# One kernel, two orders: engines that issue in the order of the text, and a triangular solve that moves to GpSimd while VectorE rounds the weights

## The chip, the core and the metric

The kernel runs on one core of a Trainium2 chip. That core has five engines that work side by side and meet at semaphores: TensorE (PE; its weight loads are shown as PEld), VectorE (DVE), ScalarE (ACT), GpSimd (POOL) and SyncE (SP), which here only issues DMA transfers. ACT issues some too. The metric is the device time of one execution in microseconds (us), as the median of several runs. Lower is better.

## What is computed

The first part is a recurrence over time, for 4 batches and 8 heads with 768 steps and 40 channels, that keeps a 40 x 40 state per batch and head. The second part is a feed-forward layer (FFN) over the 3072 tokens that come out of it, 320 to 2048 to 320 channels, with a squared ReLU.

```python
for t in range(S):                                    # B=4, H=8, S=768, D=40
    y[:, :, t] = einsum('bhd,bhde->bhe', rt, state)
    Sa = einsum('bhde,bhe->bhd', state, at)
    state_decay = state * wt[:, :, None, :] - einsum('bhd,bhe->bhde', Sa, bt)
    state = state_decay + einsum('bhd,bhe->bhde', vt, kt)
x = y.transpose(0, 2, 1, 3).reshape(B * S, H * D)     # 3072 x 320
h = maximum(x @ w_in, 0.0)                            # w_in 320 x 2048
out = (h * h @ w_out).astype(float32)                 # w_out 2048 x 320
```

The two weights arrive in 64 bits and are rounded to 32 bits in the kernel, with integer operations on VectorE.

## The kernel before

**Chunks and rounds.** Time is cut into chunks of 128 steps, so that a batch has 6 chunks and all batches 24. The kernel goes through them with the chunk number outside and the batch inside: chunks 0 to 3 are the first chunk of each of the four batches and are called round 0 here, chunks 4 to 7 are round 1, and so on to round 5. Within a chunk, the recurrence becomes matrix products and the inverse of a triangular matrix per head; between chunks of one batch only the state is carried.

**Four kinds of work.** `early(i)` (L224 to L246) prepares a chunk: transposes of w, b and a on PE (`turn`, L202), running products of the decays on VectorE (L229, L230) with their reciprocals (L232, L233), the decayed b and a (L238, L239), and a product `N` of the two (L77) that ACT copies (L244). Everything it makes is written to DRAM, by DMAs of SP (`kept_up`, `kept_down`, `kept_a`, `kept_n`). `solve(c)` (L250 to L275) makes the triangular inverses of a whole round at once. It loads the two 64 x 64 diagonal blocks of N of every head into `half_n`, with one DMA for 8 heads (16 DMAs in all, L262), so that each of 128 partitions holds half a problem. Then come 63 steps of two element-wise operations (a product L268 and a subtraction L270), each step needing the one before, and two DMAs write the result to `kept_t` (L274). `rest(i)` (L278 to L316) prepares what a chunk needs just ahead of its turn: it reads the kept decays and `a` back (L283 to L288), transposes k, r and v, makes the masked products A and RV (L218), and loads the inverse `T` (two DMAs, L314) and a block of `N` (L315). `chain(i)` (L322 to L399) is the serial part: it scales the state by four small VectorE operations (L329 to L332), transposes it on PE (L336), and goes through some seven matmul groups with ACT copies between them, then updates the state (L376) and writes the output `tokens` (L395). Four small DMAs (L398) bring the last heads' channels together. Before that, `load(i)` has SP fetch k, r, v and b (L113).

**The FFN.** `ffn()` takes the tokens of two chunks at once (a group), 12 groups in all. A group has 16 steps of three matmuls 128x256 (`ps_f<-tokens,w_in`), each followed by a ReLU on ACT (L415) and a product on VectorE (L416, `hid`), and 8 steps of four matmuls 128x320 (`ps_f<-w_out,hid`). A group's steps fill the time of PE between the links of the chain of the next two chunks.

**Rounding the weights.** `rounded` (L153 to L172) fetches a piece of 64-bit weights through ACT's DMA queue (L158) into one of two buffers, after POOL has cleared it where the piece doesn't fill it (L156), and turns it into 32 bits with 9 VectorE operations (L163 to L172). There are 24 pieces of 128x256 for `w_in` and 16 of 128x320 for `w_out`.

**Order.** The text makes four early chunks, then solve(0) on VectorE woven with the early work of chunks 4 to 7, then solve(1) on POOL, and then the loop over chunks. In a loop turn, the steps of chain(i), rest(i+1), early(i+8) and the FFN are emitted in turns by `weave`. After the last chunk of round c comes solve(c+2) on POOL. The order of the text is not the order of issue: each engine's instructions are sorted by a scheduler before the program is built. A DMA that SP issues waits at its place in SP's order for its data and its buffer, and what stands behind it waits too.

Of the kernel before, what the change touches and what calls it, by code (L numbers as in the profile page):

```python
# [17 lines left out]
def kernel(  # L18
# [22 lines left out]
    nc = tc.nc  # L41
    B, H, S, D = r.shape
# [96 lines left out]
    middle = lambda t_: t_[:, :, MID:MID + 1]  # L139
    ups = Ring("up", 1, [128, NP, C + 2], 1.0, middle)  # L140
    downs = Ring("down", 1, [128, NP, C + 2], 1.0, middle)
    minus_x = Ring("minus_x", 2, [128, H, DP], 0.0, pads)
    states = Ring("state", B, [128, NP, 2, DP], 0.0, lambda t_: t_)

    w_in = single("w_in", [128, NT, DFF])
    w_out = single("w_out", [128, NF, DM])

# [4 lines left out]
    def rounded(dst, srcs):  # L152
        raw = work.tile([128, WP, 2], I32, tag="raw", name="raw")[:, :dst.shape[-1]]  # L153
        n = 128
        if sum(m_ for _, m_, _ in srcs) < n:
            nc.gpsimd.memset(raw, 0)  # L156
        for row, m_, src in srcs:
            nc.scalar.dma_start(out=raw[row:row + m_].rearrange("p f e -> p (f e)"), in_=src.bitcast(I32))  # L158
        lo, hi = raw[:, :, 0].bitcast(U32), raw[:, :, 1]
        power = work.tile([128, WP], I32, tag="power", name="power", bufs=1)[:n, :dst.shape[-1]]  # L160
        p_ = work.tile([128, WP], I32, tag="signed", name="signed", bufs=1)[:n, :dst.shape[-1]]
        bits = dst.bitcast(I32)
        nc.vector.tensor_scalar(power, hi, 20, 0x7FF, Alu.logical_shift_right, Alu.bitwise_and)  # L163
# [4 lines left out]
        nc.vector.tensor_scalar(bits, hi, 0xFFFFF, 3, Alu.bitwise_and, Alu.logical_shift_left)  # L168
# [5 lines left out]
    WP = 320  # L174
    WI = 256
# [350 lines left out]
```

## Time and profile before

| What | Value |
|---|---|
| Three runs | 1544.03, 1536.1 and 1532.33 us, median 1536.1 |
| The profiled execution: its own time | 1534.04 us |
| The profiled execution: its span in the trace | 1532.3 us |
| Mean granted PE clock | 0.786 of full speed |
| DMA traffic | 123.01 MB, mean 80 GB/s |
| Solves on POOL | 315 products and 315 subtractions (5 solves of 63 steps) |

The span is the time from the first to the last instruction of the profiled execution; its own time is 1.7 us longer. In the profile, "busy" is the time in which an engine has an instruction in work. A line with 40 digits shows the busy share of an engine in 40 slices of the span, 38.3 us each, in tenths. A row of the timeline gives the start, the duration, the engine, the line of the code, the operation, its output and inputs, and, in brackets, the idle time of the engine just before it and what ended it. "SPq" is the time in which SP issues a DMA. The table of windows gives the busy time of each engine in a stretch, with the number of its instructions, then the granted PE clock, the busy share of the DMA engines and their GB/s.

### The profile page before, as it was taken

How to read it: one execution, taken by the hardware profiler on the slowest of the kernel's cores; microseconds unless marked ns; L12 is line 12 of the kernel's file. 1: busy time of each engine (PE TensorE's matmuls, PEld its weight loads, DVE VectorE, ACT ScalarE, POOL GpSimd, SP SyncE). 2: the span in 40 equal slices, each digit the busy share in tenths (PEclk: the TensorE clock that was granted, in tenths of full speed). 3: DMA queues.
4: the chain of work that ended last, by engine and by line, in shares of the span. 5: the costliest groups of instructions: out<-in, count | busy, mean ns of one | idle time of the engine just before them, and what ended most of it. 6: DMA issues, size and time to landing. Idle time of an engine off the chain costs nothing.

```text
span 1532.3 us, 18790 instructions
## 1 busy us (share of the span) xinstructions
PE 1062.4 (69%) x7248; PEld 884.2 (58%) x7248; DVE 598.7 (39%) x1330; ACT 202.1 (13%) x453; POOL 566.7 (37%) x702
## 2 busy tenths in 40 slices
PE   3300025009975989649989769899399994499999
PEld 2200014008854878537878658788278784388877
DVE  5887699604623243212135321346031342022311
ACT  0000001001210211101202101112012111021211
POOL 2110000009990079920199700499500899100000
PEclk9555555556897996859967878959799887699999
DMA  9634694374606677063846185654447640422100
GB/s 172 153 69 88 100 163 89 62 58 88 111 1 125 64 133 130 0 114 64 90 85 116 25 135 61 79 112 77 84 81 61 102 77 2 79 63 50 29 11 9
DMA packets 389881, 123.01 MB, mean 80 GB/s; under 512 B 318752, under 2 KB 372896, under 8 KB 389792
## 3 DMA queue, kind: packets, MB, share of 16 engines
q1 hardware_dynamic: 384000, 111.32, 45.6%
q10 hardware_dynamic: 5792, 10.49, 3.1%
q8 instruction: 57, 0.93, 0.3%
q14 instruction: 32, 0.26, 0.1%
HBM read 79.00 MB, written 41.78 MB: 79 GB/s over the span
## 4 chain that ended last, share of the span: by engine, by line
POOL 36%; PE 32%; DMA 11%; DVE 10%; SPq 7%; issue 4%; ACTq 0%; ACT 0%; DVEq 0%; POOLq 0%
PE ps_f L77 19%; POOL half_t L270 19%; POOL half_p L268 17%; PE ps_c L77 8%; PE ps_w L77 2%; DMA raw<-in_moe_w_in_dram 2%; SPq L262 2%; DMA in_k<-in_k_dram 2%; DMA raw<-in_moe_w_out_dram 2%; DVE half_t L270 2%; DVE half_p L268 2%; PE ps_w L202 2%; SPq L274 1%; SPq L398 1%; DMA kept_down<-down 1%
## 5 line engine op out<-in xcount | busy, mean ns | idle before, releaser
L268 POOL TENSOR_TENSOR half_p<-half_n,half_t 128x462 f32<-128x462 f32 (+46 forms) x315 | 255.6, 811 | 397.3 <-DMA in_k<-in_k_dram 176.1
L270 POOL TENSOR_TENSOR half_t<-half_t,half_p 128x462 f32<-128x462 f32 (+46 forms) x315 | 281.7, 894 | 24.7
L77 PE MATMUL ps_f<-tokens,w_in 128*128 128x256 f32 x1152 | 288.3, 399 | 0.5 <-DVE hid L416 0.5
L77 PEld LDWEIGHTS ps_f<-tokens,w_in 128*128 128x128 f32 x1152 | 217.7, 197 | 34.0 <-issue 1.5
L77 PE MATMUL ps_f<-w_out,hid 128*128 128x320 f32 x768 | 220.7, 441 | 0.0
L416 DVE TENSOR_TENSOR hid<-ps_f,hid 128x256 f32<-128x256 f32 x192 | 81.2, 423 | 319.2 <-ACT hid L415 319.0
L77 PEld LDWEIGHTS ps_f<-w_out,hid 128*128 128x128 f32 x768 | 144.4, 192 | 57.4 <-issue 3.0
L202 PE MATMUL ps_w<-ident,in_k 128*128 128x128 f32 x96 | 20.1, 342 | 151.0 <-DMA in_k<-in_k_dram 150.9
L77 PE MATMUL ps_c<-xr,T 64*64 64x40 f32 x768 | 65.8, 249 | 81.4 <-DMA T<-kept_t 74.5
L415 ACT ACTIVATE hid<-ps_f 128x256 f32<-128x256 f32 x192 | 73.6, 383 | 346.5 <-PE ps_f L77 346.5
L77 PEld LDWEIGHTS ps_c<-xr,T 64*64 64x64 f32 x768 | 59.1, 159 | 96.4 <-DMA T<-kept_t 75.0
L202 PEld LDWEIGHTS ps_w<-ident,in_k 128*128 128x128 f32 x96 | 14.2, 178 | 155.0 <-DMA in_k<-in_k_dram 117.7
L202 PE MATMUL ps_w<-ident,in_w 128*128 128x128 f32 x96 | 22.2, 376 | 113.9 <-DMA in_w<-in_w_dram 109.6
L77 PE MATMUL ps_w<-aT,bT 40*128 40x128 f32 x384 | 41.1, 352 | 76.3 <-DVE aT L239 76.3
L229 DVE TENSOR_TENSOR_SCAN up<-ps_w,ones 128x64 f32<-128x64 f32 x96 | 26.2, 273 | 170.9 <-PE ps_w L202 169.3
L253 POOL MEMSET half_t<- 128x2048 f32 x5 | 9.0, 1809 | 217.2 <-DMA kept_t<-half_t 217.2
L77 PEld LDWEIGHTS ps_w<-aT,bT 40*128 40x128 f32 x384 | 33.7, 244 | 86.0 <-issue 75.8
L202 PEld LDWEIGHTS ps_w<-ident,in_w 128*128 128x128 f32 x96 | 16.4, 199 | 115.5 <-issue 111.2
L244 ACT COPY N<-ps_w 128x512 f32<-128x512 f32 x48 | 25.8, 589 | 351.0 <-PE ps_w L77 284.0
L376 DVE TENSOR_TENSOR state<-ps_c,state 128x320 f32<-128x320 f32 x20 | 9.8, 491 | 126.2 <-PE ps_c L77 126.2
L218 DVE TENSOR_TENSOR RV<-ps_w,upper 128x512 f32<-128x512 f32 x48 | 30.9, 683 | 64.1 <-PE ps_w L77 64.1
L77 PEld LDWEIGHTS ps_c<-in_v,A 128*128 128x128 f32 x384 | 52.6, 215 | 2.4 <-ACT kvT L297 1.0
(182 smaller groups left out, 1475.2 us busy)
## 6 DMA issues: line engine op xcount, KB each, us to landing
kept_n<-N SPq DMA_DIRECT2D x48, 256.0 KB
half_n<-kept_n SPq DMA_DIRECT2D x96, 128.0 KB
kept_down<-down SPq DMA_DIRECT2D x24, 258.0 KB
kept_up<-up SPq DMA_DIRECT2D x24, 258.0 KB
kept_a<-aT SPq DMA_DIRECT2D x24, 256.0 KB
down<-kept_down SPq DMA_DIRECT2D x24, 256.0 KB
up<-kept_up SPq DMA_DIRECT2D x24, 256.0 KB
kept_t<-half_t SPq DMA_DIRECT2D x12, 512.0 KB
```

The source lines that it names most:

```text
L77: nc.tensor.matmul(o, l_, r_, start=start, stop=True, skip_group_check=True)
L202: nc.tensor.transpose(p_[:, q * 128:(q + 1) * 128], pair(x_, q), ident)
L218: nc.vector.tensor_tensor(t_, p_, over4(upper), Alu.mult)
L229: nc.vector.tensor_tensor_scan(up[:, q, MID + 1:C + 1], wT[:, q, MID:], ones, 1.0, Alu.mult, Alu.mult)
L244: nc.scalar.copy(t_, p_)
L262: nc.sync.dma_start(out=ns[at:at + H], in_=kept_n[c * B + bb][rows, :, rows].rearrange("s h t -> h s t"))
L268: eng.tensor_tensor(p_, ns[:, s, s + 1:].unsqueeze(1).to_broadcast([128, n, m_]), ts[:, :n, s:s + 1].to_broadcast([128, n, m_]), Alu.mult)
L270: eng.tensor_tensor(ts[:, :n, s + 1:], ts[:, :n, s + 1:], p_, Alu.subtract)
L274: nc.sync.dma_start(out=dst, in_=ts[par * 64:(par + 1) * 64])
L398: nc.sync.dma_start(out=t_[row:row + m_, j], in_=t_[at:at + m_, NT])
L415: nc.scalar.activation(h_, p_, Act.Relu)
L416: nc.vector.tensor_tensor(h_, p_, h_, Alu.mult)
```

## The change

Six things change together.

- `tc.manual_schedule()` is on: every engine issues in the order of the text. The text itself is rewritten accordingly: `early` and `rest` are cut into more pieces, the first eight early chunks overlap by hand, and the FFN gets 13 steps in each chunk instead of 12.
- All six solves run on POOL. solve(0) stands behind the early work of chunks 0 to 3, and solve(1) behind rest(0) and the first part of the weights.
- The diagonal blocks of N are written by head to a place of their own (`kept_d`, four DMAs a chunk, L275), so that a solve loads them with four DMAs (L293) and not 16. The result goes out by one DMA that POOL issues itself (L302, `kept_t`), and a chunk loads its T with four DMAs (L344) and not two.
- The decays are written and read back with all 130 columns in one piece per partition, in two buffers each instead of one. Two VectorE copies (L319 in `rest`, L408 in `chain`) stand where two small DMAs loaded `ends`.
- The rounding has 8 operations (L180 to L188) instead of 9, and `w_in` goes in 12 pieces of 128x512. Their raw data and scratch lie in the place of `w_out`, which is filled later. VectorE does the clearing (L170).
- All of `w_in` and 4 pieces of `w_out` are rounded ahead of the loop, while POOL solves round 0. The other 12 pieces of `w_out` are rounded in the first two chunks of the loop. The FFN waits for them.

Line numbers of the changed kernel in this list and below are its own.

```diff
+    ctx.enter_context(tc.manual_schedule())
...
+    ups = Ring("up", 2, [128, NP, C + 2], 1.0, whole)
+    downs = Ring("down", 2, [128, NP, C + 2], 1.0, whole)
...
+    room = w_out.rearrange("p f c -> p (f c)")
+    spare = [room[:, 2 * WI * i:2 * WI * (i + 1)] for i in range(2)]
+    spare_bits = [room[:, WI * i:WI * (i + 1)].bitcast(I32) for i in (4, 5)]
...
+    def fetch_weights():
+        if not pieces:
+            return
+        dst, srcs, cleared = pieces.pop(0)
+        wide = len(pieces) >= NF
+        raw = (spare if wide else raws)[len(pieces) % 2]
+        if cleared:
+            nc.vector.memset(raw, 0.0)
...
         nc.vector.tensor_scalar(power, hi, 20, 0x7FF, Alu.logical_shift_right, Alu.bitwise_and)
+        nc.vector.tensor_scalar(bits, hi, 0xFFFFF, 3, Alu.bitwise_and, Alu.logical_shift_left)
         nc.vector.tensor_scalar(power, power, 896.0, 1151.0, Alu.max, Alu.min)
         nc.vector.tensor_scalar(power, power, 896.0, float(1 << 23), Alu.subtract, Alu.mult)
-        nc.vector.tensor_scalar(p_, hi, -(1 << 31), None, Alu.bitwise_and)
-        nc.vector.tensor_tensor(p_, p_, power, Alu.bitwise_or)
-        nc.vector.tensor_scalar(bits, hi, 0xFFFFF, 3, Alu.bitwise_and, Alu.logical_shift_left)
-        nc.vector.tensor_tensor(bits, bits, p_, Alu.bitwise_or)
+        nc.vector.scalar_tensor_tensor(p_, hi, -(1 << 31), power, Alu.bitwise_and, Alu.bitwise_or)
         rest = power.bitcast(FP32)
         nc.vector.scalar_tensor_tensor(rest, lo, 2.0 ** -52, p_.bitcast(FP32), Alu.mult, Alu.mult)
+        nc.vector.tensor_tensor(bits, bits, p_, Alu.bitwise_or)
         nc.vector.tensor_tensor(dst, dst, rest, Alu.add)
...
+    for j in range(NT):
+        for f in range(0, DFF, WI):
+            srcs = [(row, n, moe_w_in[o:o + n, f:f + WI]) for j_, row, o, n in places if j_ == j]
+            pieces.append((w_in[:, j, f:f + WI], srcs, f < 2 * WI and sum(n for _, n, _ in srcs) < 128))
+    pieces += [(w_out[:, f, :], [(0, 128, moe_w_out[f * 128:(f + 1) * 128, :])], False) for f in range(NF)]
...
+                fetch_weights()
+                if fetched:
+                    rounded(*fetched.pop(0))
...
+    kept_d = [dram.tile([B, 2, H, HC, HC], FP32, tag=f"d{c}", name=f"kept_d{c}") for c in range(NCH)]
...
+        nc.sync.dma_start(out=kept_up[i], in_=up)
+        nc.sync.dma_start(out=kept_down[i], in_=down)
...
-            nc.sync.dma_start(out=kept_n[i][:, e * NP:(e + 1) * NP, :], in_=t_)
+            heads = slice(e * NP, (e + 1) * NP)
+            for half in range(2):
+                rows = slice(half * HC, (half + 1) * HC)
+                nc.sync.dma_start(out=kept_d[c][bb, half, heads].rearrange("h s t -> s h t"), in_=t_[rows, :, rows])
+            nc.sync.dma_start(out=kept_n[i][:, heads, :], in_=t_[:HC, :, HC:])
...
+        blocks = kept_d[c].rearrange("b f h s t -> (b f h) s t")
-                    nc.sync.dma_start(out=ns[at:at + H], in_=kept_n[c * B + bb][rows, :, rows].rearrange("s h t -> h s t"))
-                    at += H
+            for n_, part in enumerate(ns):
+                nc.sync.dma_start(out=part[par * 64:(par + 1) * 64], in_=blocks[:, n_ * Q:(n_ + 1) * Q, n_ * Q:])
...
-        for par in range(2):
-            dst = kept_t[c].rearrange("b f h (j two) t -> (b f h) two j t", two=2)[:, par]
-            nc.sync.dma_start(out=dst, in_=ts[par * 64:(par + 1) * 64])
+        nc.gpsimd.dma_start(out=kept_t[c].rearrange("two b f h j t -> (two b f h) (j t)"), in_=flat)
...
-            nc.sync.dma_start(out=ends[:, 1], in_=kept_up[i][:, :, C])
+        nc.sync.dma_start(out=up, in_=kept_up[i])
...
+        nc.vector.tensor_copy(ends, down[:, :, 0])
...
+        nc.sync.dma_start(out=g["N"], in_=kept_n[i])
         for half in range(2):
-            nc.sync.dma_start(out=g["T"][half * HC:(half + 1) * HC], in_=kept_t[c][bb, half].rearrange("h j t -> j h t"))
+            for par in range(2):
+                nc.sync.dma_start(out=g["T"][half * HC + par:(half + 1) * HC:2],
+                                  in_=kept_t[c][par, bb, half].rearrange("h j t -> j h t"))
...
+            nc.vector.tensor_copy(ended[bb], g["up"][:, :, C])
...
-            while gi not in gathered:
+            while gi not in gathered or len(pieces) + len(fetched) > NF:
...
+            while pieces or fetched:
+                yield False
...
+    firsts = [prepare(i) for i in range(LEAD)]
+    for i in range(LEAD + 1):
+        if i == 0:
+            next(firsts[0]), next(firsts[0])
+            continue
+        now, then = firsts[i - 1], firsts[i] if i < LEAD else iter(())
+        next(now)
+        next(then, None)
+        next(now)
+        next(then, None)
+        run(now)
+        if i == B:
+            run(solve(0, nc.gpsimd))
     ready = {0: {}}
-    run(several(range(B), prepare))
     load(0)
-    weave((solve(0, nc.vector), HC + 1), (several(range(B, LEAD), prepare), 4 * B))
+    first = rest(0, ready[0])
+    for _ in range(6):
+        next(first)
+    if moe_w_in.dtype != FP32:
+        fetch_weights()
+    run(weights(len(pieces) + len(fetched) - NF))
+    run(weights(NF // 4))
+    run(first)
     run(solve(1, nc.gpsimd))
-    run(rest(0, ready[0]))
     for i in range(len(order)):
         bb, c = order[i]
         parts = [(chain(i, ready.pop(i)), 10)]
...
         if i + LEAD < len(order):
-            parts.append((prepare(i + LEAD), 4))
-        if pieces:
-            parts.append((weights(20), 20))
-        parts.append((filler(PER_CHUNK), PER_CHUNK))
+            parts.append((prepare(i + LEAD), 5))
+        if pieces or fetched:
+            n = -(-(len(pieces) + len(fetched)) // (GB - i))
+            parts.append((weights(n), n))
+        parts.append((filler(STEPS // GB + 1), STEPS // GB + 1))
```

Three places show how the order moves. The first is SP in the kernel before, at the end of a chunk of round 1. `kept_t_233<-half_t` writes the result of the solve of round 2, `T<-kept_t_232` loads the inverse of the next chunk, and `in_k` is the input of the chunk after that:

```order
L314 DMA T<-kept_t_232 64x8x64
L274 DMA kept_t_233<-half_t 2048x1x64 x2
L240 DMA kept_a_173<-aT 128x512
L314 DMA T<-kept_t_232 64x8x64
L315 DMA N_3913<-kept_n_142 64x8x64
L398 DMA tokens<-tokens 24x128
L398 DMA tokens<-tokens 16x128
L398 DMA tokens<-tokens 24x128
L398 DMA tokens<-tokens 16x128
L113 DMA in_k_84<-in_k_dram 128x8x40
```

The same engine in the changed kernel, at the end of the last chunk of round 0 (`kept_t_248` is round 1's result, `half_n` the load for solve(2)):

```order
L428 DMA tokens<-tokens 16x128
L266 DMA kept_a_186<-aT 128x512
L461 DMA out_dram<-o 128x320
L341 DMA N_2478<-kept_n_149 64x512
L344 DMA T<-kept_t_248 32x8x64 x4
L275 DMA kept_d_171<-N 64x4x64 x2
L276 DMA kept_n_156<-N 64x4x64
L275 DMA kept_d_171<-N 64x4x64 x2
L276 DMA kept_n_156<-N 64x4x64
L293 DMA half_n_2504<-kept_d_171 64x2048
L293 DMA half_n_2505<-kept_d_171 64x32x32
L293 DMA half_n_2504<-kept_d_171 64x2048
L293 DMA half_n_2505<-kept_d_171 64x32x32
L114 DMA in_k_87<-in_k_dram 128x8x40
```

The write of `kept_t` is gone from SP's order (it stands in POOL's own, behind the solve's last subtraction). What waits for a solve on SP now is the T loads, and `half_n` and `in_k` stand behind them.

The second place is VectorE where the solve of round 0 begins, before; `w_out`, `signed`, `power` and `raw` belong to the last piece of weights:

```order
L169 TENSOR_TENSOR w_out<-w_out,signed 128x320
L171 SCALAR_TENSOR_TENSOR power<-raw,signed 128x320
L172 TENSOR_TENSOR w_out<-w_out,power 128x320
L268 TENSOR_TENSOR half_p<-half_n,half_t 128x63
L270 TENSOR_TENSOR half_t<-half_t,half_p 128x63
```

In the changed kernel the solve isn't on VectorE. Behind the early work and rest(0) (its last products L335) stand the weight pieces:

```order
L335 TENSOR_TENSOR in_k_86<-ps_w,in_k_86 128x8x40
L335 TENSOR_TENSOR in_b_90<-ps_w,in_b_90 128x8x40
L170 MEMSET w_out 128x1024 x2
L180 TENSOR_SCALAR w_out<-w_out 128x512
L181 TENSOR_SCALAR w_in<-w_out 128x512
L182 TENSOR_SCALAR w_out<-w_out 128x512
L183 TENSOR_SCALAR w_out<-w_out 128x512
L184 SCALAR_TENSOR_TENSOR w_out<-w_out 128x512
L186 SCALAR_TENSOR_TENSOR w_out<-w_out 128x512
L187 TENSOR_TENSOR w_in<-w_in,w_out 128x512
L188 TENSOR_TENSOR w_in<-w_in,w_out 128x512
```

So 40 pieces that stood ahead of the first solve now stand, 16 of them, behind work that only needs the early chunks, and the rest behind the start of the loop.

The third place is PE in the changed kernel, where one chunk ends and a new FFN group begins (`ps_c<-RX` is the chunk's last product, `ps_f<-tokens` the group's first, `ident,state` the transpose of the scaled state of the next chunk):

```order
L78 MATMUL ps_c<-RX,in_b_91 64x128 x8
L78 MATMUL ps_f<-w_out,hid 128x320 x4
L332 MATMUL ps_w<-ident,down 128x128 x4
L78 MATMUL ps_w<-aT,bT 128x128 x8
L78 MATMUL ps_f<-tokens,w_in 128x256 x3
L366 MATMUL ps_c<-ident,state_131 128x128 x4
L78 MATMUL ps_f<-tokens,w_in 128x256 x3
```

And VectorE there; `f` and `state` are the small operations that scale the state (L359 to L362):

```order
L335 TENSOR_TENSOR in_b_90<-ps_w,in_b_90 128x8x40
L446 TENSOR_TENSOR hid<-ps_f,hid 128x256
L359 TENSOR_TENSOR f<-end_7329,ends 128x4
L360 COPY f<-f 128x4
L361 TENSOR_TENSOR f<-f,same 128x8
L362 TENSOR_TENSOR state_131<-state_131,f 128x8x40
L446 TENSOR_TENSOR hid<-ps_f,hid 128x256 x2
```

In the kernel before, the scheduler placed nine FFN matmuls (`ps_f`) between `ps_c<-RX` and the state's transposes at one such place. Now one step of three stands ahead of the transposes, and on VectorE its `hid` product stands ahead of the four small operations.

More of the change, by code (lines that the diff above doesn't have):

```diff
@@ L145 @@
     w_in = single("w_in", [128, NT, DFF])
     w_out = single("w_out", [128, NF, DM])
[L152 to L156, printed above, removed]
-        for row, m_, src in srcs:
[L158 to L161, printed above, removed]
+    WI = 512
@@ L180, in load_weights @@
[L180 to L193 removed]
+    pieces = []
@@ L194 @@
+    kept_n = [dram.tile([HC, H, HC], FP32, tag=f"n{i}", name=f"kept_n{i}") for i in range(len(order))]
+    kept_d = [dram.tile([B, 2, H, HC, HC], FP32, tag=f"d{c}", name=f"kept_d{c}") for c in range(NCH)]
     kept_a = [dram.tile([128, NP, C], FP32, tag=f"a{i}", name=f"kept_a{i}") for i in range(len(order))]
@@ L450, in weave @@
             run(gen)
-    def several(n, f):
-        for i in n:
-            if i < len(order):
-                yield from f(i)
     def prepare(i):
```

100 lines of the change are left out of this document (46 added, 54 removed).

## The prediction

> **What bounds the kernel now.** I read the page's totals and slices first, then the waits, then the stages between the solves.
>
> ```profile
> span 1532.3 us, 18790 instructions
> PE 1062.4 (69%) x7248; PEld 884.2 (58%) x7248; DVE 598.7 (39%) x1330; ACT 202.1 (13%) x453; POOL 566.7 (37%) x702
> PE   3300025009975989649989769899399994499999
> PE ps_w L202 <- DMA in_k<-in_k_dram: 150.9, 5, 39.5
> ```
>
> PE is busy for 1062 of 1532 us, and the slices say where it isn't: the first ten (383 us), and a dip about every 200 us later on. The dips are the five waits for `in_k`, 150.9 us together. SP's timeline and PE's at the second of them show what it is:
>
> ```profile
> 603.42 0.65 SPq L314 DMA_DIRECT2D T<-kept_t  x1
> 658.65 2.71 SPq L274 DMA_DIRECT2D kept_t<-half_t  x2
> 670.06 0.53 SPq L113 DMA_DIRECT2D in_k<-in_k_dram  x1
> 673.12 1.08 PE L202 MATMUL ps_w<-ident,in_k 128*128 128x128 f32 x4 [35.08 <-DMA in_k<-in_k_dram]
> ```
>
> SP issues nothing from 604 to 658: it stands at the write of the running solve's result, and the input of a later chunk is queued behind it. By stages (us, then PE, PEld, DVE, ACT, POOL, granted clock, DMA share, GB/s):
>
> ```profile
> 0.00:198.00 198.00, 28.77 (x152) 22.45 (x152) 147.87 (x426) 6.65 (x11) 18.96 (x57) 0.61 0.66 118
> 198.00:344.00 146.00, 28.99 (x168) 25.19 (x168) 89.78 (x195) 5.98 (x11) 2.11 (x3) 0.52 0.60 89
> 344.00:461.00 117.00, 100.22 (x782) 86.75 (x782) 48.49 (x91) 20.04 (x45) 107.16 (x126) 0.81 0.34 66
> 542.00:659.00 117.00, 90.37 (x674) 75.75 (x672) 42.55 (x82) 17.55 (x39) 106.82 (x126) 0.81 0.45 82
> 659.00:757.00 98.00, 82.35 (x528) 68.74 (x529) 20.68 (x42) 15.76 (x37) 2.11 (x3) 0.83 0.59 88
> 1341.00:1484.00 143.00, 143.00 (x1094) 118.18 (x1092) 36.70 (x71) 28.95 (x67) 0.00 (x0) 1.00 0.17 40
> ```
>
> Up to 198 VectorE rounds the weights; up to 344 it solves round 0, and loads follow. Only then does the chain over the chunks start. From there solve and loads alternate, with POOL idle between solves (659 to 757); only the last stage has PE busy throughout, at full clock. So the kernel is bound by VectorE for 198 us, by solve and loads for 146, and then by PE with five holes.
>
> **Part 1: the holes.** `kept_t` leaves SP's order, so nothing ahead of `in_k` waits for the running solve. The T loads wait for the solve before it, and they stand ahead of the next solve's loads. At 344 it was such loads that POOL waited for:
>
> ```profile
> 331.82 2.57 SPq L262
> 339.91 4.06 DMA T<-kept_t
> 344.04 0.29 POOL L268 TENSOR_TENSOR half_p<-half_n,half_t 128x63 f32<-128x63 f32 x1 [38.82 <-DMA T<-kept_t]
> 460.82 0.27 POOL L270 TENSOR_TENSOR half_t<-half_t,half_p 128x32 f32<-128x32 f32 x1
> L268 DVE TENSOR_TENSOR half_p<-half_n,half_t x63: 212/560/696, 197.8 to 292.9; 128x462 f32<-128x462 f32 x3, 128x62 f32<-128x62 f32 x2, 128x120 f32<-128x120 f32 x2, 128x174 f32<-128x174 f32 x2
> ```
>
> A solve takes 117 us on POOL (344.0 to 461.1), 95 on VectorE. With four loads and one write, and some 20 us lost to VectorE (part 2), I put POOL's cycle at 150 us. PE's work for a round is 4 x 43 = 172 (part 3), so POOL is ahead, and the 150.9 us of holes cost nothing if PE is the bound: I don't subtract them but add up PE's work.
>
> **Part 2: the start.** The early work of chunks 0 to 3 must pass the DMA engines before solve(0) starts. At 118 GB/s (first window) 6.5 MB (four chunks of 1.6 MB: w, b and a of 0.16 each, two decays and a of 0.26 each, N of 0.26 or more) take 55 us, and a chunk's own latency comes on top: 62, between 50 and 80. Alone the solve ends at 179. The rounding runs on VectorE meanwhile:
>
> ```profile
> 125.35 0.29 DVE L163 TENSOR_SCALAR power<-raw 128x256 int32<-128x256 int32 x1 [3.04 <-DMA raw<-in_moe_w_in_dram]
> 128.25 0.29 DVE L163 TENSOR_SCALAR power<-raw 128x256 int32<-128x256 int32 x1
> 158.08 0.32 DVE L168 TENSOR_SCALAR w_out<-raw 128x320 int32<-128x320 int32 x1
> 161.37 0.32 DVE L168 TENSOR_SCALAR w_out<-raw 128x320 int32<-128x320 int32 x1
> ```
>
> Nine operations on 256 columns take 2.90 us, on 320 columns 3.29. 256 further columns at the slope of 0.39 us for 64 make 4.5 for 512; with 8 of 9 operations 4.1, and 2.9 for 320: 12 x 4.1 + 4 x 2.9 = 61 us ahead of the loop, 12 x 2.9 = 35 in it. By the order it begins behind the early work of chunks 4 to 7 and most of rest(0), at about 118 (the same 6.5 MB again). But VectorE and POOL disturb each other. VectorE's small multiply without and with POOL at work, POOL's largest subtraction without and with VectorE:
>
> ```profile
> 248.70 0.15 DVE L331 TENSOR_TENSOR f<-f,same 128x8 f32<-128x8 f32 x1
> 1254.80 0.17 DVE L330 COPY f<-f 128x4 f32<-128x4 f32 x1
> 1255.01 0.93 DVE L331 TENSOR_TENSOR f<-f,same 128x8 f32<-128x8 f32 x1
> 1255.97 0.49 DVE L332 TENSOR_TENSOR state<-state,f 128x320 f32<-128x320 f32 x1
> 397.67 1.17 POOL L270 TENSOR_TENSOR half_t<-half_t,half_p 128x510 f32<-128x510 f32 x1
> 1255.99 1.49 POOL L270 TENSOR_TENSOR half_t<-half_t,half_p 128x510 f32<-128x510 f32 x1
> ```
>
> An operation of 0.15 us took 0.93, ending when POOL's did, and POOL's next took 0.32 longer beside one of 0.49. So each operation with two inputs in SBUF waits for one of POOL's, about 0.8 us, and delays the next by about 0.33. From 118 some 72 of POOL's 126 operations remain: 72 x 0.33 = 24, and solve(0) ends at 203. Of the rounding's 8 operations four have two SBUF inputs: 64 of them, 0.8 us each, are 51 us, so it ends at 118 + 61 + 51 = 230, and chunk 0 follows at 232. Bounds: 191 with no disturbance (179, then 12 for write and loads), 245 with every one of the 128 operations paying 0.5.
>
> [...]
>
> Chunks 0 and 1 then run with 12 pieces of `w_out` on VectorE and solve(1) on POOL. VectorE's own work is 12 us a chunk (48.49 in the window 344 to 461, four chunks), so 24 + 35, some 60, alone; 48 rounding operations and some 25 others at 0.8 bring 118. Bounds 60 and 138; I take 120, since nothing but VectorE holds these chunks and the FFN. Chunk 2 starts at 352.
>
> **Part 3: PE from there.**
>
> ```profile
> 1490.76 20.88 PE L77 MATMUL ps_f<-tokens,w_in 128*128 128x256 f32 x96
> 1511.48 17.39 PE L77 MATMUL ps_f<-w_out,hid 128*128 128x320 f32 x64
> 1426.91 0.60 PE L336 MATMUL ps_c<-ident,state 128*128 128x128 f32 x4
> 1458.07 0.60 PE L336 MATMUL ps_c<-ident,state 128*128 128x128 f32 x4
> 1341.31 1.01 PE L77 MATMUL ps_c<-in_v,in_k 128*128 128x80 f32 x8
> 825.59 1.16 PE L77 MATMUL ps_w<-aT,bT 40*128 40x128 f32 x16
> ```
>
> An FFN group takes 38.3 us (38.1 and a lead-in), 12 groups 459. A chunk of the last round lasts 31.16 (1426.91 to 1458.07) with 72 FFN matmuls of 0.2175, 15.7, in it: 15.5. Other rounds add the state's growth (1.0), and early work adds 1.16 and three sets of transposes at 0.60, together 3.0. From chunk 2: 459 + 2 x 15 + 16 x 16.5 + 4 x 15.5 + 14 x 3.0 = 857 at full clock.
>
> **Part 4: holes that the new order makes.** Two, seen in the third place of the order. The tokens of a group's second chunk go through four DMAs before the group can start:
>
> ```profile
> 1452.51 0.69 DVE L395 TENSOR_TENSOR tokens<-ps_c,up 128x512 f32<-128x512 f32 x1 [1.96 <-PE ps_c L77]
> 1453.23 2.88 SPq L398 DMA_DIRECT2D tokens<-tokens  x4
> L415 ACT ACTIVATE hid<-ps_f 128x256 f32<-128x256 f32 x192 | 73.6, 383 | 346.5 <-PE ps_f L77 346.5
> ```
>
> 0.69 + 2.88 + 2 to land is 5.6, of which about 2 lie beside other matmuls: 3.7 a group, 12 x 3.7 = 44. Then the state's four operations stand behind `hid`: 0.38 and 0.42, then 2.3 with POOL at work (to 1256.46 from about 1254.2, the rows above), a hole of 3.5 where a solve runs (14 chunks), of 2.2 elsewhere (6): 62. Bounds 0, if other matmuls happen to stand there, and twice that, for both kinds. Holes cost clock as well:
>
> ```profile
> 778.59 2.08 PE L77 MATMUL ps_w<-aT__4484,kvT 40*128 40x128 f32 x16 [3.83 <-DVE kvT L291]
> ```
>
> After a hole of 3.83 us, 16 matmuls took 2.08 where the same shape took 1.16 at 825.59: half clock, for up to 47 us. Where FFN matmuls follow it is shorter: 659 to 757 has 0.83, so 33 us at half, 14 of them the rest of the hole, 19 behind it, a loss of 9.5 at most. With 0 to 9.5 for 12 group starts (0 to 114), I take 40.
>
> [...]
>
> **The sum.** 352 + 857 + 44 + 62 + 40, and 3.4 behind the last matmul (1528.9 to 1532.3) and 1.7 outside the span: 1360. It is made against the profiled execution's 1534.0, 2.1 below the median of 1536.1, less than the bounds of any term.
>
> **The rivals.** (a) No lock: rounding and solve overlap freely. Chunk 0 at 191, chunks 0 and 1 in 60, holes of 2.2: 191 + 60 + 857 + 44 + 44 + 40 + 5 = 1241. For it: half of the rounding's operations have one input, and many of the pairs could miss each other. Against: 0.93 against 0.15. (b) SP in stated order becomes the bound, and the kernel slower. A chunk now has about 30 transfers on SP. At 0.53 each (670.06) that is 16 us and hidden; where transfers crowd, one took eight times that:
>
> ```profile
> 531.62 4.24 SPq L113 DMA_DIRECT2D in_k<-in_k_dram  x1
> ```
>
> With PE at 43 us a chunk it decides from 1.45 us a transfer. At 1.75, 52 us a chunk, 22 chunks add 22 x 9 = 198: 1558. Against it: DMAs are busy 0.45 of the time at the mean solve stage, and fewer, larger transfers lower that. (c) Half clock lasts 43 us after each of 12 group starts, as it did at 778: 12 x 21.5 = 258 in place of 40: 1578. Against: the 0.83 above. That the change doesn't do what it says is excluded by the order: on SP and VectorE it stands as stated.
>
> **How the numbers follow.** The forecast gets 0.67, (a) 0.20, (b) 0.07, (c) 0.06. The time is 1360. The range reaches down to (a) with a little room, 1230, and up to the forecast's own high bounds (114 of clock for 40, 138 and 245 in part 2): 1360 + 74 + 31, about 1460, which also holds the doubled holes without the rest (106); (b), (c) and what lies outside are less than 2 in 10. A measurement of this kernel can tell about 1%, as its three runs spread by 0.8%. Slower: most of (b) and (c), which at half their price still lie below 1521, so 0.09; within 1%: 0.03; faster: 0.88.
>
> **What would show it.** Right: solve(0) on POOL from about 62 to 203; rounding operations of 0.8 us and more beside it; chunk 0's first product at 232 and chunk 2's at 352; no wait of PE for `in_k` over 5 us; waits of PE for `tokens` and for the state's scaling at 3 to 4 us; a granted clock of 0.9 from 400 on. Wrong: solve(0) ending below 185 (no lock); SP issuing without a pause through a round (b); windows at 0.5 to 0.7 with FFN matmuls in them (c); or POOL's cycle above 172 us, with T late in every round.

## The result, and the profile after

The changed kernel takes 1451.1 us (median of four runs, 1440.9 to 1460.3) against 1535.9 for the kernel before: ratio 0.944, 95% interval 0.937 to 0.951. It is faster, as forecast, by 85 us; the forecast was 176. The profiled execution took 1453.09 us with a span of 1451.4.

The page after: span, busy time by engine, and the slices of PE (36.3 us each).

```profile
span 1451.4 us, 18536 instructions
...
PE 1049.5 (72%) x7248; PEld 865.5 (60%) x7248; DVE 591.8 (41%) x1095; ACT 201.6 (14%) x453; POOL 687.7 (47%) x815
...
PE   5340000016699689898998998989968989899999
```

From the twelfth slice on PE is nearly full, and the five deep dips of the kernel before are gone; two slices with a 6 are left, at 472 and 1052 us. But PE stands still in slices 4 to 8. The start in four stages, and the rest as one (PE, PEld, DVE, ACT, POOL, granted clock, DMA share, GB/s):

```profile
122.00:190.00 68.00, 0.00 (x0) 0.00 (x0) 0.04 (x1) 0.00 (x0) 51.33 (x63) 0.50 0.16 36
190.00:322.00 132.00, 0.00 (x0) 0.00 (x0) 123.95 (x115) 0.06 (x1) 116.33 (x110) 0.50 0.28 62
322.00:406.00 84.00, 57.92 (x407) 51.70 (x408) 64.67 (x152) 8.97 (x18) 11.15 (x21) 0.62 0.42 115
406.00:1451.00 1045.00, 940.29 (x6555) 771.74 (x6553) 337.49 (x715) 181.37 (x416) 438.99 (x517) 0.91 0.38 75
```

From 122 to 190 nothing works but POOL; VectorE, which was to round the weights then, has one instruction. From 190 to 322 VectorE and POOL work side by side. Chunk 0 starts at 322, chunk 2 at 406. The waits that tell why (total us, times, longest):

```profile
PE ps_c L78 <- ACT xr L378: 215.0, 1, 215.0
...
DVE w_out L180 <- DMA w_out<-in_moe_w_in_dram: 76.8, 4, 68.2
...
PE ps_c L366 <- DVE state L362: 47.9, 20, 3.3
...
PE ps_w L226 <- DMA in_k<-in_k_dram: 37.1, 7, 10.5
...
PE ps_f L78 <- DMA tokens<-tokens: 25.3, 19, 3.0
```

PE's 215 us are the wait for chunk 0's first copy on ACT, at 321.94, which is queued behind the weight transfers that ACT issues (the last three ahead of it from 306.21 to 321.90). Of VectorE's wait for raw data 68.2 us are one wait. The timelines of ACT's queue, POOL, SP and VectorE around it:

```profile
107.70 3.00 ACTq L172 DMA_DIRECT2D w_out<-in_moe_w_in_dram  x3
...
182.69 2.01 ACTq L172 DMA_DIRECT2D w_out<-in_moe_w_in_dram  x4
```

```profile
175.35 0.72 POOL L302 DMA_DIRECT2D kept_t<-half_t  x1 [0.31 <-POOL half_t L300]
```

```profile
179.69 2.58 SPq L344 DMA_DIRECT2D T<-kept_t  x4
```

```profile
190.19 0.43 DVE L180 TENSOR_SCALAR w_out<-w_out 128x512 int32<-128x512 int32 x1 [68.15 <-DMA w_out<-in_moe_w_in_dram]
```

ACT issues its sixth transfer by 111 and the seventh, the third of the second piece, only at 183, after solve(0) has been written (175.35) and SP has issued the four T loads of chunk 0 (179.69). ACT has nothing to do with the solve. The built program, shown with the semaphores that an instruction waits for, holds the link. First the four transfers of the second piece on ACT, then the T loads on SP:

```
L172 DMA w_out<-in_moe_w_in_dram 40x1024 [waits DMAHW7_49,DVE_49]
L172 DMA w_out<-in_moe_w_in_dram 40x1024 [waits DMAHW1_49]
L172 DMA w_out<-in_moe_w_in_dram 24x1024 [waits DMAHW2_49]
L172 DMA w_out<-in_moe_w_in_dram 16x1024 [waits DMAHW4_49]

L344 DMA T<-kept_t_247 32x8x64 [waits DMAHW0_49,DMASW0_49]
L344 DMA T<-kept_t_247 32x8x64 [waits DMAHW2_49]
L344 DMA T<-kept_t_247 32x8x64 [waits DMAHW4_49]
L344 DMA T<-kept_t_247 32x8x64 [waits DMAHW6_49]
```

In this program all transfers of SP and ACT share eight semaphores (`DMAHW0` to `DMAHW7`). The piece's third and fourth transfer wait on `DMAHW2` and `DMAHW4`, as the second and third T load do, and the first T load waits for solve(0) (`DMASW0` is the write of `kept_t`). I read it so that the two transfers wait until those T loads have landed. The times fit, with ACT going on 3.00 us after SP began to issue the T loads (182.69 and 179.69), and e1 tests it: with those loads off these semaphores the wait of 68.15 us is 7.29.

The second thing to see is what the rounding costs beside solve(1). VectorE, then POOL, in the same three microseconds:

```profile
266.48 1.36 DVE L180 TENSOR_SCALAR w_out<-w_out 128x512 int32<-128x512 int32 x1
...
269.00 1.43 DVE L182 TENSOR_SCALAR w_out<-w_out 128x512 int32<-128x512 int32 x1
...
277.79 1.37 DVE L180 TENSOR_SCALAR w_out<-w_out 128x512 int32<-128x512 int32 x1
```

```profile
267.64 1.16 POOL L298 TENSOR_TENSOR half_p<-half_n,half_t 128x527 f32<-128x527 f32 x1
268.87 1.27 POOL L300 TENSOR_TENSOR half_t<-half_t,half_p 128x527 f32<-128x527 f32 x1
270.22 1.13 POOL L298 TENSOR_TENSOR half_p<-half_n,half_t 128x510 f32<-128x510 f32 x1
```

In these rows the two engines alternate, one operation each. The operation that took 0.43 us alone at 190.19 takes 1.36, and a piece (266.48 to 277.79) 11.3 us.

### The profile page after: what moved, and what is told of

Same layout as the page of the kernel before. It is cut to its first block, busy times and chain, and to the rows that moved or that the text cites. A ratio compares the mean times of both kernels' runs of the same rounds, so it can differ in the third digit from the quotient of the medians.

```text
span 1451.4 us, 18536 instructions
## 1 busy us (share of the span) xinstructions
PE 1049.5 (72%) x7248; PEld 865.5 (60%) x7248; DVE 591.8 (41%) x1095; ACT 201.6 (14%) x453; POOL 687.7 (47%) x815
## 2 busy tenths in 40 slices
DMA packets 300104, 116.91 MB, mean 81 GB/s; under 512 B 270192, under 2 KB 275184, under 8 KB 298480
## 4 chain that ended last, share of the span: by engine, by line
PE 63%; DVE 15%; POOL 8%; DMA 8%; SPq 3%; issue 2%; ACT 1%; DVEq 0%; POOLq 0%; ACTq 0%
PE ps_f L78 34%; PE ps_c L78 16%; PE ps_w L78 6%; POOL half_t L300 4%; PE ps_w L226 4%; POOL half_p L298 4%; DMA in_k<-in_k_dram 2%; DMA half_n<-kept_d 1%; DMA tokens<-tokens 1%; PE ps_c L366 1%; SPq L428 1%; DVE w_in L187 1%; DVE w_out L184 1%; DVE w_out L186 1%; DMA kept_a<-aT 1%
## 5 line engine op out<-in xcount | busy, mean ns | idle before, releaser
L298 POOL TENSOR_TENSOR half_p<-half_n,half_t 128x462 f32<-128x462 f32 (+19 forms) x378 | 316.2, 836 | 465.3 <-DMA half_n<-kept_d 436.1
L300 POOL TENSOR_TENSOR half_t<-half_t,half_p 128x462 f32<-128x462 f32 (+19 forms) x378 | 346.8, 917 | 29.6
L78 PE MATMUL ps_f<-tokens,w_in 128*128 128x256 f32 x1152 | 322.3, 427 | 25.9 <-DMA tokens<-tokens 25.3
L78 PEld LDWEIGHTS ps_f<-tokens,w_in 128*128 128x128 f32 x1152 | 232.6, 213 | 69.1 <-issue 21.4
L78 PEld LDWEIGHTS ps_c<-in_v,A 128*128 128x128 f32 x384 | 66.0, 259 | 3.0 <-issue 0.2
L78 PE MATMUL ps_c<-in_v,A 128*128 128x40 f32 x384 | 63.0, 337 | 0.0
L318 DVE TENSOR_TENSOR kvT<-ps_w,down 128x512 f32<-128x512 f32 x24 | 16.6, 691 | 101.6 <-DMA down<-kept_down 91.5
L242 DVE TENSOR_TENSOR A<-ps_w,upper 128x512 f32<-128x512 f32 x48 | 30.9, 685 | 61.6 <-PE ps_w L78 61.6
L366 PE MATMUL ps_c<-ident,state 128*128 128x128 f32 x80 | 17.7, 361 | 47.9 <-DVE state L362 47.9
L242 DVE TENSOR_TENSOR RX<-ps_w,upper 128x512 f32<-128x512 f32 x48 | 30.9, 685 | 51.2 <-PE ps_w L78 51.2
L226 PE MATMUL ps_w<-ident,in_k 128*128 128x128 f32 x96 | 20.0, 343 | 37.1 <-DMA in_k<-in_k_dram 37.1
L366 PEld LDWEIGHTS ps_c<-ident,state 128*128 128x128 f32 x80 | 11.3, 178 | 57.8 <-DVE state L362 45.6
```

What stands on the lines that cost most here:

```text
L78: nc.tensor.matmul(o, l_, r_, start=start, stop=True, skip_group_check=True)
L226: nc.tensor.transpose(p_[:, q * 128:(q + 1) * 128], pair(x_, q), ident)
L242: nc.vector.tensor_tensor(t_, p_, over4(upper), Alu.mult)
L298: eng.tensor_tensor(p_, ns[s // Q][:, s % Q, s % Q + 1:].unsqueeze(1).to_broadcast([128, n, m_]), ts[:, :n, s:s + 1].to_broadcast([128, n, ...
L300: eng.tensor_tensor(ts[:, :n, s + 1:], ts[:, :n, s + 1:], p_, Alu.subtract)
L318: nc.vector.tensor_tensor(kT, turn(x_["k"]), down[:, :, 1:C + 1], Alu.mult)
```

## The experiments

All times are medians of four runs, each with the kernel before on the same chip; the ratio is to that one. All but the seventh start from the changed kernel.

**e1_free_slots: the shared semaphores.** The T loads of chunk 0 and the loads of solve(1) go to POOL's queue.

```diff
-                nc.sync.dma_start(out=part[par * 64:(par + 1) * 64], ...
+                (nc.gpsimd if c == 1 else nc.sync).dma_start(out=part[par * 64:(par + 1) * 64], ...
...
-                nc.sync.dma_start(out=g["T"][half * HC + par:(half + 1) * HC:2],
+                (nc.gpsimd if i == 0 else nc.sync).dma_start(out=g["T"][half * HC + par:(half + 1) * HC:2],
```

> In the changed kernel VectorE waits 68 us (122 to 190) for the raw data of the second weight piece, and the DMA engines stand still meanwhile. Theory A: the transfers of ACT's queue and of SP's share eight semaphores, and the piece's third and fourth transfer wait for the T loads of chunk 0, which have the same semaphores and wait for solve(0). Here those T loads and the loads of solve(1) are issued by POOL, which has its own semaphores. A expects no wait over 10 us for raw data, weight pieces during solve(0) at up to 11 us each, chunk 0's first copy at 235 to 260 us instead of 322, and 1365 to 1390 us in all. Rival B: the piece waits for its buffer or for VectorE's own progress, not for a transfer on SP: the wait of 68 us stays, 1440 to 1460 us.

1404.8 us, ratio 0.913 (0.910 to 0.916), 46 less than the changed kernel. VectorE's wait at the first piece, the end of solve(0) on POOL, ACT's first copy of chunk 0, and the two stages that follow it:

```profile
114.67 0.58 DVE L180 TENSOR_SCALAR w_out<-w_out 128x512 int32<-128x512 int32 x1 [7.29 <-DMA w_out<-in_moe_w_in_dram]
```

```profile
187.08 0.72 POOL L302 DMA_DIRECT2D kept_t<-half_t  x1 [0.31 <-POOL half_t L300]
```

```profile
241.15 0.42 ACT L378 COPY xr<-ps_c 64x320 f32<-64x320 f32 x1 [140.17 <-DVE bits L186]
```

```profile
241.00:361.00 120.00, 57.27 (x399) 51.30 (x400) 103.43 (x142) 7.97 (x16) 86.58 (x91) 0.54 0.28 76
361.00:1401.00 1040.00, 927.35 (x6566) 760.20 (x6562) 341.31 (x725) 182.62 (x418) 439.06 (x517) 0.92 0.39 76
```

The wait of 68 us is gone, and chunk 0 starts 81 us earlier, where A put it. B falls. The total is 15 us above A's range, because 36 of the 81 us come back at once: chunks 0 and 1 now take 120 us instead of 84, since solve(1) and the last 12 pieces fall together (POOL is busy for 86.58 of the 120 us, and for 11.15 of the 84).

**e2_no_solve1: the price of the exclusion.** This kernel leaves out the 63 steps of solve(1), so its round 1 isn't the reference's computation.

```diff
-        for s in range(HC - 1):
+        for s in range(HC - 1 if c != 1 else 0):
```

> Leaves out the 63 steps of solve(1), so that round 1's inverse is only its start value; POOL then stands idle while VectorE rounds 14 of the 16 pieces, which takes 11.3 us a piece of 512 columns beside POOL and took 4.3 us (190.2 to 194.5) beside none. Theory A, POOL and VectorE exclude each other: pieces at 4.3 us and 3.0 us throughout, chunk 0's first copy at 250 to 265 us instead of 322, some 60 us gained, 1385 to 1395 us. Rival B, the pieces wait for their transfers: a piece stays at 8 us or more, with waits of VectorE for raw data between pieces, and at most 20 us are gained.

1387.9 us, ratio 0.902 (0.897 to 0.906). The rounding beside an idle POOL, and the first copy of chunk 0:

```profile
246.11 0.43 DVE L180 TENSOR_SCALAR w_out<-w_out 128x512 int32<-128x512 int32 x1
...
250.49 0.43 DVE L180 TENSOR_SCALAR w_out<-w_out 128x512 int32<-128x512 int32 x1
```

```profile
263.71 0.42 ACT L378 COPY xr<-ps_c 64x320 f32<-64x320 f32 x1 [163.04 <-DVE w_out L187]
```

4.38 us a piece, as the prediction had it for VectorE alone (4.1), where the changed kernel took 11.3 beside solve(1). Chunk 0 starts 58 us earlier and the whole is 63 us shorter. A holds: it is POOL's work that makes the pieces long, not their transfers.

**e3_scale_early: the state's scaling.** The four operations L359 to L362 move into `rest`, behind the k and b products of the turn before.

```diff
         if c > 0:
-            f_ = new("f", [128, NP, 2], 2)
-            nc.vector.tensor_tensor(f_[:, :, 0], ended[bb], g["ends"], Alu.mult)
...
         g["v"] = x_["v"]
+        st = states.tiles[bb]
+        if c > 0:
+            f_ = new("f", [128, NP, 2], 2)
+            nc.vector.tensor_tensor(f_[:, :, 0], ended[bb], g["ends"], Alu.mult)
...
         yield
```

> The four small operations that scale the state move from the start of a chunk to the turn before it (behind the k and b products). Theory A: PE's 20 waits for them, 47.8 us together, go, and part of the half-clock time behind them (90 us of excess PE time in all, 20 x 2 us taken): 1365 to 1405 us. Rival B: PE then waits for what was hidden behind them (ACT's copy, the A products, the tokens), so that under 20 us are gained: 1430 us or more.

1410.8 us, ratio 0.919 (0.915 to 0.923), between A and B. The 20 waits went, but a new one grew from 37.1 to 78.9 us, while the granted clock rose:

```profile
PE ps_w L226 <- DMA in_k<-in_k_dram: 78.9, 16, 13.3
```

```profile
406.00:1408.00 1002.00, 897.94 (x6558) 737.04 (x6556) 338.78 (x719) 181.56 (x416) 439.61 (x517) 0.95 0.40 79
```

So nothing was won in waiting; the 40 us are PE's busy time, 940 to 898. When PE no longer stops at a chunk's start, it is early for `in_k`, which stands on SP behind the tokens, the T loads and the blocks of N, and at the longest waits (up to 13.3 us) behind the loads of a solve.

**e4_scale_early_lag: the tokens too.** As e3, and two FFN steps of a group run at the start of the next two chunks.

```diff
-    def filler(n):
-        for _ in range(n):
-            next(second, None)
+    def filler(i, n):
+        for s in range(n):
+            if s != n // 2 and not (i == GB and s < 2):
+                next(second, None)
             yield
```

> As e3_scale_early, and the FFN lags two of its 24 steps behind, so that the last two steps of a group stand at the start of the next two chunks, where PE waits for the tokens. Theory A: 18 waits for tokens, 25 us, go as well, and with them most of what is left of half clock: 1330 to 1380 us, a granted clock above 0.95 from 420 us on. Rival B: the half clock doesn't come from these short waits: the excess of PE time stays at 70 us or more, 1385 us or more.

1366.6 us, ratio 0.889 (0.886 to 0.891), as A had it. The clock from chunk 2 on is 0.97, PE's busy time 875 us:

```profile
413.00:1362.00 949.00, 875.36 (x6525) 724.54 (x6524) 335.43 (x710) 180.81 (x414) 440.34 (x517) 0.97 0.42 82
```

```profile
PE ps_w L226 <- DMA in_k<-in_k_dram: 64.9, 14, 10.4
```

The short waits did cost clock: with both kinds gone, 65 us of PE's busy time went with them (940 to 875), and B falls.

**e5_all_three.** e4 with e1's transfers and the loads of all later solves on POOL's queue.

```diff
+                (nc.gpsimd if c > 0 else nc.sync).dma_start(out=part[par * 64:(par + 1) * 64], ...
```

> e4_scale_early_lag with the T loads of chunk 0 and the loads of all solves but the first on POOL's queue. Theory A, that three causes add up (shared semaphores at the start, 46 us; state scaling and tokens, 85 us; loads of a solve ahead of in_k on SP, five waits of 7 to 10 us): 1451 - 46 - 85 - 25, 1280 to 1320 us. Rival B, that the start's gain is lost again once PE is full: 1340 us or more.

1333.6 us, ratio 0.869 (0.867 to 0.871): 33 us less than e4, between A and B. The wait for `in_k` fell to 31.2 us, and a wait for the decays behind it on SP came forward (`kvT` waits for `down`):

```profile
PE ps_w L78 <- DVE kvT L318: 63.5, 10, 11.2
...
PE ps_w L226 <- DMA in_k<-in_k_dram: 31.2, 10, 8.4
```

From chunk 2 on, the four long ones of these waits (8.1 to 11.2 us) each come just behind the loads of a solve, which POOL now issues. At the first, POOL issues them from 452.8, and SP issues `down` from 454.3; the DMA engines are busy throughout from 452 to 470 (a share of 1.10), and PE goes on at 470.1. That these loads still hold up what PE needs, by traffic now and not by their place in the queue, is my guess from these times; no run shows it.

**e6_no_manual: the stated order alone undone.**

```diff
-    ctx.enter_context(tc.manual_schedule())
```

> The changed kernel without the stated order: the scheduler sorts each engine again. Theory A, that the five waits for in_k of the kernel before (150.9 us) went because kept_t is written from POOL's queue and the solve has four loads, whatever the order: the five waits stay below 60 us together, 1400 to 1480 us. Rival B, that the stated order itself removed them: waits of 20 to 40 us for in_k come back at the ends of solves, 1500 us or more.

1343.4 us, ratio 0.876 (0.874 to 0.878): 108 us faster than with the stated order. Neither theory had this. A is right on the five waits, of which one of 30.9 us is left, but its time was too long by 57 us or more:

```profile
PE ps_f L77 <- DVE hid L445: 112.1, 8, 35.9
...
PE ps_c L77 <- DMA T<-kept_t: 40.7, 1, 40.7
...
PE ps_w L225 <- DMA in_k<-in_k_dram: 30.9, 1, 30.9
```

```profile
225.00:317.00 92.00, 61.94 (x397) 55.21 (x398) 84.54 (x105) 7.90 (x17) 85.65 (x82) 0.52 0.40 92
```

The scheduler lets the rounding begin among the early chunks. Chunk 0's T arrives at 220, and the FFN starts at 317. It has holes of its own, three of 34 to 36 us at FFN steps.

**e7_before_write_on_pool: one part alone.** The kernel before, with its write of `kept_t` issued by POOL.

```diff
-            nc.sync.dma_start(out=dst, in_=ts[par * 64:(par + 1) * 64])
+            nc.gpsimd.dma_start(out=dst, in_=ts[par * 64:(par + 1) * 64])
```

> The kernel before, its own order, with the two writes of kept_t issued by POOL instead of SP. Theory A, that SP standing at this write was what made PE wait for in_k: most of the 150.9 us go, 1400 to 1460 us. Rival B, that the next thing on SP that needs the solve (T loads, the 16 loads of the next solve, whose buffer is free only when this solve ends) takes its place: waits for in_k or T of over 80 us together stay, 1490 to 1540 us.

1473.3 us, ratio 0.961 (0.958 to 0.964), between the two. The waits for `in_k` fell from 150.9 to 88.0 us:

```profile
PE ps_w L202 <- DMA in_k<-in_k_dram: 88.0, 4, 38.7
```

```profile
634.93 0.50 SPq L113 DMA_DIRECT2D in_ab<-in_a_dram  x1
663.14 0.30 SPq L262 DMA_DIRECT2D half_n<-kept_n  x1
...
672.07 1.98 SPq L113 DMA_DIRECT2D in_k<-in_k_dram  x1
```

SP now stands from 635 to 663 at the next solve's first load, whose buffer is the running solve's, with `in_k` still behind it. Moving the write took away 62.9 of the 150.9 us; for the rest, the loads of the next solve took its place, as B says.

**e8_solve1_late.** e5 with solve(1) behind chunk 1 in the text and its loads on ACT's queue.

```diff
-    run(solve(1, nc.gpsimd))
     for i in range(len(order)):
...
         weave(*parts)
+        if i == 1:
+            run(solve(1, nc.gpsimd))
```

> e5_all_three with solve(1) behind the first two chunks in the text, its loads on ACT's queue behind the last raw weights, so that POOL rests while VectorE rounds the last 21 pieces. Theory A, exclusion of VectorE and POOL sets the time of chunks 0 and 1: they take 55 to 75 us instead of some 130, chunk 0 starts at 215 to 230; round 1's inverse is then late and PE waits 30 to 60 us for T once; in sum 10 to 40 us less than e5_all_three. Rival B: chunks 0 and 1 are bound by their own chain and by ACT's queue, they take 100 us or more, and the time is that of e5_all_three or more.

1318.4 us, ratio 0.859 (0.857 to 0.861), the fastest of all. Chunks 0 and 1 and the wait for round 1's T:

```profile
219.00:311.00 92.00, 60.76 (x434) 55.44 (x435) 63.00 (x155) 9.67 (x20) 0.00 (x0) 0.59 0.49 111
```

```profile
PE ps_c L78 <- DMA T<-kept_t: 41.6, 2, 37.9
```

With POOL idle, chunks 0 and 1 take 92 us where they took 128 (240 to 368) in e5: more than A's 55 to 75, so a part is their own chain. Chunk 2 starts 57 us earlier, but behind it 37.9 us go to one wait for the late T.

**e9_all_three_no_manual.** e5 without the stated order (the line of e6).

> e5_all_three without the stated order. The changed kernel without it took 1343 us, 108 us less than with it. Theory A, that the stated order loses only by its three faults (shared semaphores at the start, the late state scaling, the group start), which e5_all_three removes: then the scheduler has nothing left to gain, 1330 us or more. Rival B, that the scheduler's order is better as such: 1310 us or less.

1338.8 us, ratio 0.874 (0.871 to 0.877), against e5's 0.869 (0.867 to 0.871). A holds: without its three faults the stated order is no worse than the scheduler's, and hardly better.

**e10_half_width.** e5 with each rounding operation cut in two.

```diff
+    def rounded(dst, raw, scratch):
+        n = dst.shape[-1] // 2
+        for e in range(2):
+            cols = slice(e * n, (e + 1) * n)
+            rounded_half(dst[:, cols], raw[:, 2 * e * n:2 * (e + 1) * n], [t_[:, cols] for t_ in scratch])
```

> e5_all_three with every rounding operation cut into two of half the columns, so that VectorE does the same elements in twice the operations. Theory A, that each VectorE operation beside a solve waits for one operation of POOL, long or short: alone a piece of 512 columns would go from 4.4 to some 6 us, beside POOL from 11.3 to 18 or more; the first copy of chunk 0 moves from 240 to 290 us or later, the rounding in chunks 0 and 1 takes longer too, 1390 us or more. Rival B, that the two engines share their access by elements: 28 pieces pay 1.5 us each at most, chunk 0 at 240 to 265, below 1375 us.

1373.9 us, ratio 0.895 (0.890 to 0.900). Three operations beside solve(0), and chunk 0's first copy:

```profile
140.70 0.28 DVE L187 TENSOR_SCALAR w_in<-w_out 128x256 int32<-128x256 int32 x1
...
142.02 1.12 DVE L189 TENSOR_SCALAR w_out<-w_out 128x256 int32<-128x256 int32 x1
143.17 1.13 DVE L190 SCALAR_TENSOR_TENSOR w_out<-w_out 128x256 int32<-128x256 int32 x1
```

```profile
304.00 0.42 ACT L386 COPY xr<-ps_c 64x320 f32<-64x320 f32 x1 [203.19 <-DVE bits L192]
```

Half as wide, seven of the eight operations still take 0.9 to 1.4 us from 115 to 162, about as long as one of POOL's (0.91 to 1.18 from 139 to 150). The second of the eight, L187, is hardly ever held up (0.28 us), and no run shows why. A piece of 512 columns takes up to 17.6 us, near A's 18. Chunk 0 starts 64 us later than in e5, as A said (290 or later, B 265 at most). The whole lost only 40 us, below A's 1390 and within B's 1375: solve(1) ends at 318, 14 us behind chunk 0's start, where in e5 it ends 92 us behind it, so most of the last pieces are rounded beside an idle POOL. So chunk 0's start speaks for A, and the total decides nothing.

## Why the prediction was right in direction and wrong in size

The terms of its sum, against the trace after:

| Term | Forecast | Measured |
|---|---|---|
| Start of chunk 0 | 232 | 322 |
| Chunks 0 and 1 | 120 | 84 |
| PE's work from chunk 2 at full clock, and clock lost | 857 + 40 | 940 |
| Waits for the state's scaling | 62 | 47.9 |
| Waits for tokens, from chunk 2 | 44 | 25.0 |
| Waits for in_k, from chunk 2 | 0 | 26.6 |

The errors of 90, 43 and 27 us one way and of 36, 14 and 19 the other leave the 91 by which 1451 exceeds 1360. The 2 us "to land" in the 44 no trace of the kernel before shows; in the trace after, the eleven transfers of tokens in the chain that ended last took 1.64 to 2.34. That the sum isn't further off is luck. Chunks 0 and 1 were short because solve(1) was nearly over when they started (POOL is busy for 11 of their 84 us); in e1, with solve(1) beside them, they take the 120 of the forecast.

**The step that failed** is in part 2: "The rounding runs on VectorE meanwhile", during solve(0). It didn't. solve(0) began at 57 (forecast 62) and ended at 175, with one piece beside it, and all the others were rounded after it. The order of each engine's own instructions, on which I had leaned, doesn't show a wait between two queues; the waits of the built program do. e1 shows this step as the cause of the late start: with the link cut, chunk 0 starts at 241 and chunk 2 at 361, against the forecast's 232 and 352. The kernel gains 46 of the 91 us by it; the rest is mostly clock and the waits for `in_k`. That 241 lies so near 232 is in part luck: pieces took up to 11.2 us beside solve(0), but solve(0) ended at 187 and not at 203, and three pieces fell between the two solves, two of them at 4.3 us. "solve(0) ending below 185" was named as the sign of no disturbance at all; here it was the sign that almost nothing ran beside it.

**The disturbance** is there, as forecast (a piece takes 11.3 us beside solve(1) and 4.38 beside an idle POOL, e2), and its size was off. I let half of the rounding's operations wait, those with two SBUF inputs, an estimate from one product of 0.93 us and one copy of 0.17 beside POOL. In the changed kernel all eight wait, those with one included (1.36 us for 0.43), and no trace shows why. A piece takes 11.3 us, and not the 4.1 + 4 x 0.8 of my sum, 7.3. What POOL loses was put too high: 12 us in e1 (solve(0) ends at 187 and not at 175), with 24 forecast. Rival (a), no disturbance, is out by e2 and e10.

**Clock.** 83 us above 857 instead of 40. I gave a loss of clock to 12 group starts. It is lost behind half of the 20 waits for the state too (ten have transposes of 1.07 to 1.12 us behind them), here after waits of 3.30 and 2.03 us:

```profile
597.32 1.09 PE L366 MATMUL ps_c<-ident,state 128*128 128x128 f32 x4 [3.30 <-DVE state L362]
598.20 2.44 PE L78 MATMUL ps_f<-tokens,w_in 128*128 128x256 f32 x6
...
603.11 0.60 PE L226 MATMUL ps_w<-ident,in_w 128*128 128x128 f32 x4
603.55 1.46 PE L78 MATMUL ps_f<-tokens,w_in 128*128 128x256 f32 x6
...
637.69 1.07 PE L366 MATMUL ps_c<-ident,state 128*128 128x128 f32 x4 [2.03 <-DVE state L362]
638.55 2.74 PE L78 MATMUL ps_f<-tokens,w_in 128*128 128x256 f32 x6
```

Four transposes and six FFN matmuls take up to 1.9 times their time of 603; the granted clock is 0.54 from 597.30 to 600.40 and from 637.60 to 641.30, and 1.00 from 603.10 to 606.00. The length of a wait alone doesn't decide it: of the waits of 1.93 or 1.94 us two were followed by transposes of 1.11 us and eight by transposes of 0.66, and one of 3.04 by 0.63. The 83 us spread over the 43 waits behind 406 (20, 18 and 5) are 1.9 us for each on average. The forecast counted 12 holes at 3.3; there were over three times as many, each cheaper. That it is clock and not more work shows in the product: 940 us at a granted clock of 0.91 are some 856 at full clock, beside the forecast's 857. That the waits are the cause is shown by e4, where two of the three kinds are gone and 65 of the 83 us with them.

**What was right.** The holes for `in_k` are gone as a bound, though not, as forecast, all below 5 us: five are left from chunk 2 on, the two longest of 9.3 and 10.5 us, each where a solve's loads stand just ahead of `in_k` on SP. PE's work is the 857 (e4, at a clock of 0.97, has 875), and both new kinds of holes are where the order showed them, each somewhat shorter than forecast. Rival (b), SP in stated order, didn't decide here, but it stood next in line: e3 woke it (37.1 to 78.9 us), and with the loads of the solves off SP it fell again (64.9 in e4, 31.2 in e5). The traffic did go down, as the case against it had it: the DMA queues' packets took 49.1% of the 16 engines' span before and 39.7% after (389881 and 300104 packets). Rival (c), half clock for 43 us, is out: the clock was back at 1.00 some 6 us after the wait at 597.

**Where the gain came from and where it went.** The change without its stated order is 192 us faster than before (e6), the stated order takes 108 of them back. e1 to e5 name what it takes: the shared semaphores, the late scaling, the group's start; without them the stated order does as well as the scheduler's (e9). How the 192 divide among the solves on POOL, the blocks by head, the write from POOL, the decays and the rounding was tried for the write alone (e7, 62 us in the kernel before); the rest stays open.

## What to carry to other kernels

Before trusting that two queues overlap, look at what each transfer waits for in the built program: here two transfers on ACT that shared semaphores with loads behind a solve were the start of a wait of 68 us, which was 7 without that link (e1). VectorE work beside a long GpSimd loop on SBUF was held up in nearly each of its operations here (a piece took 11.3 us in place of 4.4, and up to 17.6 in twice as many operations, e10), so it should be few and wide operations, or lie elsewhere. Where PE is the bound, look at short waits for what they cost in clock as well, here 100 us as waits and 83 as clock, and for the waits that they hide (for `in_k` 37.1 us, and 78.9 when the 20 waits for the state went, e3).

## What the runs showed of the hardware that was not expected

- A `tensor_scalar` with one SBUF input was held up beside GpSimd as an operation with two was: L180 took 0.43 us alone and 1.36 beside a solve, L188 with two inputs 0.69 and 1.43; a `tensor_scalar` half as wide took 1.12 (e10). One of the eight half-wide operations hardly ever was (L187, 0.28).
- GpSimd paid far less than VectorE: in e1 solve(0) ended at 187, with rounding beside its last 72 us, against 175 without, while the pieces beside it took up to 11 us in place of 4.4.
- A wait of 2.03 us was followed by about half clock (0.54 granted, transposes of 1.07 us against 0.60), and two of 1.93 by transposes of 1.11 us; eight others of 1.93 or 1.94 were followed by 0.66.
